# Windowed attention followed by a gated feed-forward: feed-forward in chunks of 384 tokens, q and k loaded as nine rows per partition, and jobs placed by time and dependency

## The chip, the cores and the metric

The kernel runs on one core of a Trainium2 chip. The core has five engines that run their own instruction streams in order and wait for each other through semaphores: TensorE (PE, matmuls; its weight loads are listed apart as PEld), VectorE (DVE), ScalarE (ACT), GpSimd (POOL) and SyncE (SP, which here issues DMAs). Matmuls write to PSUM[...]; ScalarE and VectorE read PSUM and write SBUF. The metric is the device time of one execution in microseconds, the median of three runs; the profile is of one more execution, and its span (282.3 us) is a little shorter than that run's device time (284.04 us).

## What is computed

Eight batches of 576 tokens with 8 heads of 64 go through attention within a window of 32 tokens to each side. The result, 512 wide, goes through a feed-forward of width 1024, whose hidden layer is gated by the sigmoid of a convolution of three taps along the tokens.

```python
# q, k, v: (8, 8, 576, 64)   w_in: (512, 1024)   conv_w: (3, 1024)   w_out: (1024, 512)
scores = q @ k.T / sqrt(64); scores[|i - j| > 32] = -1e9
x      = softmax(scores) @ v                        # heads side by side: (8, 576, 512)
h      = relu(x @ w_in)                             # (8, 576, 1024)
conv   = sum_k conv_w[k] * h[:, i + k - 1]          # zero outside the 576 tokens
out    = (h * sigmoid(conv)) @ w_out                # (8, 576, 512), float32
```

## The kernel before

Inputs arrive as fp32 and are cast to bf16 by GpSimd. Per batch, q, k and v come in five blocks of 128 tokens; a row of 64 values (256 bytes) is contiguous in both places.

```python
psum = tc.tile_pool(name="psum", bufs=4, space=PSUM)          # four slots of two banks
def load_block(dst, src, b, c, lo):
    nc.sync.dma_start(dst[s0 - lo:s1 - lo, c, :, :],
                      src[b, :, s0:s1, :].rearrange("h p d -> p h d"))
# batch 0's loads are issued first; w_in (cast while it is loaded) is asked for by GpSimd after
# the casts of q and k and the first of v; then come the loads of batch 1, w_out, batch 2 ...
def load_w_in():
    for c in range(KC): nc.gpsimd.dma_start(w_in_sb[:, c, :], moe_w_in[128*c:128*c+128, :])
```

The attention of a pair of heads g (32 pairs, four per batch) is made of jobs. TensorE transposes q and k against an identity (five matmuls each), ScalarE and VectorE copy the results out; 18 small matmuls give the scores of nine query tiles of 64; ScalarE takes the exponential, VectorE multiplies by a mask; 20 matmuls multiply by v (with a column of ones, so that the sum comes along); VectorE divides; five matmuls transpose the result.

```python
def job_tr(g, which):   # q: copy by ScalarE; k: by VectorE. 128x576 each
def job_sc(g):          # scores into two slots, exp 128x576 twice, mask 128x1152 once
def job_av(g):          # 20 matmuls into one slot, reciprocal 128x10, multiply 128x640
def job_xt(g):          # 5 transposes into one slot, copy 128x576 into xT[b][:, pr, :]
```

The feed-forward works on a whole batch, in two halves of 288 tokens in the two banks of a slot:

```python
def job_ph(b, m):       # x @ w_in, one of 8 blocks m of the hidden width
    for gg in range(2):
        for kc in range(KC):      # 4
            matmul(ps[:, gg, 0:288], w_in_sb[:, kc, m*128:(m+1)*128], xT[b][:, kc, gg*288:(gg+1)*288])
    nc.scalar.activation(hT[:, m, 1:S+1], ps, Relu, scale=0.5)
def job_pc(b, m):       # the convolution: three diagonal matrices, shifted reads of hT
    for gg in range(2):
        for kk in range(3):
            matmul(ps[:, gg, 0:288], diag_w[:, kk, m, :], hT[:, m, gg*288+kk:gg*288+kk+288])
    nc.scalar.activation(tn, ps, Tanh)                     # sigmoid by way of tanh
    nc.vector.scalar_tensor_tensor(out=gT[...], in0=tn, scalar=1.0, in1=hT[:, m, 1:S+1], add, mult)
def job_py(bp, tiles):  # gated @ w_out for one or two tiles of 128 tokens of a pair of batches
    # 8 matmuls of 512 columns per tile, one ScalarE copy, one store of up to 512 KB
```

The order in which the jobs are given out is a merge: in period `per`, the attention of batch `per`, the feed-forward of batch `per - 1` and the loads of batches `per + 1` and `per + 2` are mixed in proportion.

```python
for per in range(B + 2):
    extra = lj[1] if per == 0 else lj[per + 1][cut:] ...
    extra = extra + lj[per + 2][:cut] ...
    merge(extra, att.get(per, []), ffn.get(per, []))
```

So the feed-forward of batch 0 stands in the order beside the attention of batch 1.

Of the kernel before, what the change touches and what calls it, by code (L numbers as in the profile page):

```python
# [15 lines left out]
def kernel(  # L17
# [21 lines left out]
    TG = S // 2  # L39
    PAD = 32  # L40
    AVS = 171
# [6 lines left out]
    psum = ctx.enter_context(tc.tile_pool(name="psum", bufs=4, space=bass.MemoryType.PSUM))  # L48

    NLD = 2  # L50
    qst = pp.tile([128, NBLK, H, 64], FP32, name="qst")
    kst = pp.tile([128, NBLK, H, 64], FP32, name="kst")
    vst = pp.tile([128, NBLK, H, 64], FP32, name="vst")
    qnb_pp = [pp.tile([128, NBLK, H, 64], BF16, name=f"qnb{i}") for i in range(NLD)]
    knb_pp = [pp.tile([128, NBLK, H, 64], BF16, name=f"knb{i}") for i in range(NLD)]
# [4 lines left out]
    hT_pp = [pp.tile([128, MB, S + 2], BF16, name=f"hT{i}") for i in range(2)]  # L60
# [6 lines left out]
    mask = consts.tile([128, NT, 64], BF16, name="mask")  # L67
# [3 lines left out]
    def load_block(dst, src, b, c, lo):  # L71

        s0, s1 = max(0, lo), min(S, lo + 128)
        fixed(nc.sync.dma_start(  # L74
            dst[s0 - lo:s1 - lo, c, :, :], src[b, :, s0:s1, :].rearrange("h p d -> p h d")
        ))

# [5 lines left out]
    def load_stream(b):  # L83

        i = b % NLD
        ve, vo = ve_pp[i], vo_pp[i]

        def cast_v(c):
            cast(ve[:, c, :, 0:64], vst[:, c, :, :])
            half = cast if b > 0 else nc.scalar.copy  # L90
            if c < NBLK - 1:
                half(vo[0:64, c, :, 0:64], vst[64:128, c, :, :])
            if c > 0:
                half(vo[64:128, c - 1, :, 0:64], vst[0:64, c, :, :])

        for c in range(NBLK):
            yield (lambda c=c: load_block(qst, q, b, c, 128 * c),
                   lambda c=c: cast(qnb_pp[i][:, c, :, :], qst[:, c, :, :]))
            yield (lambda c=c: load_block(kst, k, b, c, 128 * c),
                   lambda c=c: cast(knb_pp[i][:, c, :, :], kst[:, c, :, :]))  # L100
        for c in range(NBLK):
            yield (lambda c=c: load_block(vst, v, b, c, 128 * c - PAD), lambda c=c: cast_v(c))


    for st in (qst, kst):
        nc.vector.memset(st[64:128, NBLK - 1, :, :], 0.0)
# [3 lines left out]
    for ld, _ in loads0:  # L110
        ld()
    nc.scalar.dma_start(
# [4 lines left out]
    nc.vector.memset(mask, 1.0)  # L117
    nc.gpsimd.affine_select(
        out=mask, in_=mask, compare_op=ALU.is_ge, fill=0.0, base=0,
# [3 lines left out]
        out=mask, in_=mask, compare_op=ALU.is_ge, fill=0.0, base=64,  # L123
        pattern=[[0, NT], [1, 64]], channel_multiplier=-1,
    )
    nc.vector.memset(mask[0:PAD, 0, :], 0.0)
    nc.vector.memset(mask[128 - PAD:128, NT - 1, :], 0.0)
# [5 lines left out]
    for t_ in hT_pp:  # L133
        nc.vector.memset(t_[:, :, 0], 0.0)
        nc.vector.memset(t_[:, :, S + 1], 0.0)
    for kk in range(3):
        for m in range(MB):
            nc.vector.tensor_scalar(
                out=diag_w[:, kk, m, :], in0=ident,
                scalar1=conv_w_sb[:, kk, m:m + 1], scalar2=None, op0=ALU.mult,  # L140
            )

    def load_w_in():
        for c in range(KC):
            fixed(nc.gpsimd.dma_start(w_in_sb[:, c, :], moe_w_in[128 * c:128 * c + 128, :]))

    def load_w_out():
        fixed(nc.gpsimd.dma_start(w_out_sb, moe_w_out.rearrange("(c p) f -> p c f", p=128)))


    def slot():
        return psum.tile([128, 2, 512], FP32, name="ps", tag="ps")

    def flat(ps):
        return ps.rearrange("p a x -> p (a x)")
# [4 lines left out]
    def transpose_into(ps, nat):  # L160

        pf = flat(ps)
        for c in range(NBLK):
            cols = min(128, S - 128 * c)
            nc.tensor.matmul(  # L165
                pf[:, 128 * c:128 * c + cols], nat(c), ident[:, 0:cols], start=True, stop=True
            )
        return pf[:, 0:S]

    def job_tr(g, which):  # L170
        b, pr = g // NP, g % NP
        nat = (qnb_pp if which == "q" else knb_pp)[b % NLD]
        t_ = transpose_into(
            slot(), lambda c: nat[:, c, 2 * pr:2 * pr + 2, :].rearrange("p h d -> p (h d)")
        )
        if which == "q":
            qT = apool.tile([128, S], BF16, name="qT", tag="qT")
            state["q", g] = qT
            nc.scalar.copy(out=qT, in_=t_)  # L179
        else:  # L180
            kT = kT_pp[g % NKT]
            state["k", g] = kT
            nc.vector.tensor_copy(out=kT[:, PAD:PAD + S], in_=t_)

    def job_sc(g):
        qT, kT = state.pop(("q", g)), state.pop(("k", g))
        pss = [slot(), slot()]
        for t in range(NT):
            for e in range(2):
                nc.tensor.matmul(  # L190
                    flat(pss[e])[:, 64 * t:64 * t + 64],
# [4 lines left out]
        attn = apool.tile([128, 2, S], BF16, name="attn", tag="attn")  # L196
        state["a", g] = attn
        for e in range(2):
            nc.scalar.activation(attn[:, e, :], flat(pss[e])[:, 0:S], AF.Exp, bias=0.0, scale=scale)  # L199
        nc.vector.tensor_tensor(  # L200
            out=attn, in0=attn,
            in1=mask.rearrange("p t x -> p (t x)")[:, None, :].broadcast_to([128, 2, S]),
            op=ALU.mult,
        )

    def job_av(g):
# [4 lines left out]
        pf = flat(slot())  # L211
        for c in range(NBLK):
            for e in range(2):
                for j in range(2):
                    t = min(2 * c + j, NT - 1)
                    nc.tensor.matmul(  # L216
                        pf[64 * j:64 * j + 64, AVS * c + 65 * e:AVS * c + 65 * e + 65],
                        attn[:, e, 64 * t:64 * t + 64],
# [3 lines left out]
        po = pf[:, 0:AVS * NBLK].rearrange("p (c x) -> p c x", x=AVS)[:, :, 0:130].rearrange(  # L222
            "p c (e x) -> p c e x", x=65
        )
        if pr == 0:
            xn[b] = fpool.tile([128, NBLK, H, 64], BF16, name="xn", tag="xn")
        rec = apool.tile([128, NBLK, 2], FP32, name="rec", tag="rec")
        nc.vector.reciprocal(rec, po[:, :, :, 64])
        nc.vector.tensor_tensor(  # L229
            out=xn[b][:, :, 2 * pr:2 * pr + 2, :], in0=po[:, :, :, 0:64],  # L230
            in1=rec[:, :, :, None].broadcast_to([128, NBLK, 2, 64]), op=ALU.mult,
        )

    def job_xt(g):
        b, pr = g // NP, g % NP
        t_ = transpose_into(
            slot(), lambda c: xn[b][:, c, 2 * pr:2 * pr + 2, :].rearrange("p h d -> p (h d)")
        )
        if pr == 0:
            xT[b] = fpool.tile([128, KC, S], BF16, name="xT", tag="xT")  # L240
        nc.vector.tensor_copy(out=xT[b][:, pr, :], in_=t_)  # L241
# [3 lines left out]
    def job_ph(b, m):  # L245

        hT = hT_pp[b % 2]
        ps = slot()
        for gg in range(2):
            for kc in range(KC):  # L250
                nc.tensor.matmul(  # L251
                    ps[:, gg, 0:TG],
                    w_in_sb[:, kc, m * 128:(m + 1) * 128],
# [167 lines left out]
```

The softmax here doesn't subtract the row's maximum and nothing guards it: scores larger than these inputs give would overflow.

## Time and profile before

The kernel takes 284.93 us (median; 284.92 to 285.02).

| engine | busy us | share of the span | instructions |
|---|---|---|---|
| PE | 247.8 | 88% | 2880 |
| PEld | 169.4 | 60% | 2880 |
| DVE | 164.0 | 58% | 269 |
| ACT | 159.3 | 56% | 253 |
| POOL | 130.4 | 46% | 189 |

The page of the profile cuts the span into 40 slices of 7.06 us and gives the busy share of each engine in each slice, in tenths; under these it gives the share in which the 16 DMA engines were busy and how many GB/s they moved. A TensorE that is listed as busy need not stream at its peak: matmuls overlap, and the end of each is modelled. The times from one start to the next, in a stretch without waits, tell what a matmul costs. The groups of the profile give the mean duration of an instruction of one kind; the chain of work that ended last is followed back from the last instruction, and shows what each step waited for.

### The profile page before, as it was taken

Reading aid. Unit: us, or ns where it says so; the run is one execution under the profiler, and the core shown is the slowest. Engines: PE = TensorE matmul, PEld = TensorE weight load, DVE = VectorE, ACT = ScalarE, POOL = GpSimd, SP = SyncE. Lnnn points to the kernel's source line nnn. Section 1 sums busy time; section 2 is a strip of 40 time slices with the busy share of each in tenths; the row PEclk is TensorE's granted clock in tenths of the full one; section 3 lists DMA queues with packets and bytes.
Section 4 is the critical chain, followed back from the end, with each engine's and each line's share of the span. In section 5 each row is a group of like instructions: output and inputs, shape, how many; then the busy total and the mean of one; then the engine's idle time right before and its main releaser. Section 6 shows DMA issues by size and latency. Waiting matters only on the chain.

```text
span 282.3 us, 6977 instructions
## 1 busy us (share of the span) xinstructions
PE 247.8 (88%) x2880; PEld 169.4 (60%) x2880; DVE 164.0 (58%) x269; ACT 159.3 (56%) x253; POOL 130.4 (46%) x189
## 2 busy tenths in 40 slices
PE   0356649987899999999999999999999999999994
PEld 0135526765656675767676767667567765676641
DVE  4834635686657585658665865486657735752220
ACT  1059133656556665666665766567557855575532
POOL 4583579996788358244756273736353000000000
PEclk9999999999999999999999999999999999999999
DMA  9999999999968692979858966895243010202104
GB/s 109 215 202 227 203 201 202 205 175 222 206 126 217 168 199 35 219 167 199 148 146 158 218 101 144 165 226 120 69 82 104 2 77 0 90 24 78 74 2 184
DMA packets 122175, 40.30 MB, mean 143 GB/s; under 512 B 116000, under 2 KB 117024, under 8 KB 122144
## 3 DMA queue, kind: packets, MB, share of 16 engines
q1 hardware_dynamic: 117440, 37.76, 67.1%
q0 software_dynamic: 1616, 2.10, 4.4%
q10 hardware_dynamic: 3088, 0.01, 0.7%
q8 instruction: 22, 0.36, 0.6%
q14 instruction: 9, 0.07, 0.1%
HBM read 32.52 MB, written 9.44 MB: 149 GB/s over the span
## 4 chain that ended last, share of the span: by engine, by line
PE 75%; DMA 8%; ACT 7%; SPq 4%; DVE 2%; issue 1%; POOL 1%; ACTq 0%
PE ps L251 23%; PE ps L293 22%; PE ps L269 17%; PE ps L165 6%; DMA kst<-in_k_dram 5%; ACT y_sb L300 5%; SPq L74 4%; PE ps L216 3%; PE ps L190 3%; DMA vst<-in_v_dram 2%; DMA qst<-in_q_dram 2%; ACT tn L276 1%; ACT hT_87 L257 1%; DVE gT L279 1%; ACT attn L199 1%
## 5 line engine op out<-in xcount | busy, mean ns | idle before, releaser
L251 PE MATMUL ps<-xT,w_in_sb 128*128 128x288 bf16 x512 | 75.4, 291 | 3.1 <-DVE xT L241 1.2
L293 PE MATMUL ps<-w_out_sb,gT 128*128 128x512 bf16 x288 | 65.3, 379 | 0.4 <-ACT tn L276 0.4
L251 PEld LDWEIGHTS <-w_in_sb 128*128 128x128 bf16 x512 | 47.5, 99 | 16.7 <-issue 3.6
L276 ACT ACTIVATE tn<-ps 128x576 f32<-128x576 f32 x64 | 41.8, 654 | 18.3 <-PE ps L269 17.3
L293 PEld LDWEIGHTS <-gT 128*128 128x128 bf16 x288 | 27.3, 98 | 31.0 <-DVE gT L279 0.5
L300 ACT COPY y_sb<-ps 128x1024 f32<-128x1024 f32 (+1 forms) x20 | 18.5, 927 | 46.3 <-PE ps L293 46.3
L199 ACT ACTIVATE attn<-ps 128x576 bf16<-128x576 f32 x64 | 38.4, 653 | 6.1 <-PE ps L190 6.0
L269 PEld LDWEIGHTS <-diag_w 128*128 128x128 bf16 x384 | 34.1, 97 | 9.7 <-issue 1.3
L200 DVE TENSOR_TENSOR attn<-attn,mask 128x1152 bf16<-128x1152 bf16 x32 | 25.9, 810 | 23.7 <-ACT attn L199 23.6
L279 DVE SCALAR_TENSOR_TENSOR gT<-tn,hT_88 128x576 bf16<-128x576 f32 x32 | 26.5, 831 | 19.0 <-ACT tn L276 18.8
L179 ACT CAST qT<-ps 128x576 bf16<-128x576 f32 x32 | 20.1, 637 | 22.7 <-PE ps L165 22.6
L279 DVE SCALAR_TENSOR_TENSOR gT<-tn,hT_87 128x576 bf16<-128x576 f32 x32 | 28.0, 878 | 5.3 <-ACT tn L276 5.2
L269 PE MATMUL ps<-hT_87,diag_w 128*128 128x288 bf16 x192 | 29.0, 286 | 1.2 <-ACT qT L179 0.6
L269 PE MATMUL ps<-hT_88,diag_w 128*128 128x288 bf16 x192 | 29.0, 286 | 0.0
L257 ACT ACTIVATE hT_87<-ps 128x576 bf16<-128x576 f32 x32 | 21.0, 656 | 13.0 <-PE ps L251 12.3
L257 ACT ACTIVATE hT_88<-ps 128x576 bf16<-128x576 f32 x32 | 21.0, 656 | 11.9 <-PE ps L251 11.7
L229 DVE TENSOR_TENSOR xn<-ps,rec 128x640 bf16<-128x640 f32 x32 | 26.3, 822 | 0.8
L241 DVE CAST xT<-ps 128x576 bf16<-128x576 f32 x32 | 23.7, 751 | 4.4 <-PE ps L165 4.4
L79 POOL TENSOR_SCALAR vo_83<-vst 64x512 bf16<-64x512 f32 x32 | 23.9, 748 | 2.4
L79 POOL TENSOR_SCALAR knb_79<-kst 128x512 bf16<-128x512 f32 x20 | 13.7, 684 | 22.5 <-DMA kst<-in_k_dram 17.9
L216 PEld LDWEIGHTS <-attn 128*64 128x64 bf16 x640 | 14.6, 115 | 11.8 <-issue 9.5
L79 POOL TENSOR_SCALAR ve_81<-vst 128x512 bf16<-128x512 f32 x20 | 14.0, 700 | 16.6 <-DMA vst<-in_v_dram 8.4
(64 smaller groups left out, 277.2 us busy)
## 6 DMA issues: line engine op xcount, KB each, us to landing
qst<-in_q_dram SPq DMA_DIRECT2D x32, 256.0 KB, 4.9
kst<-in_k_dram SPq DMA_DIRECT2D x32, 256.0 KB, 5.4
out_dram<-y_sb SPq DMA_DIRECT2D x16, 512.0 KB, 3.4
vst<-in_v_dram SPq DMA_DIRECT2D x24, 256.0 KB, 5.2
vst<-in_v_dram SPq DMA_DIRECT2D x16, 192.0 KB, 4.8
qst<-in_q_dram SPq DMA_DIRECT2D x8, 128.0 KB, 5.1
kst<-in_k_dram SPq DMA_DIRECT2D x8, 128.0 KB, 4.8
w_in_sb<-in_moe_w_in_dram POOLq DMA_DIRECT2D x4, 256.0 KB, 6.8
```

What stands on the lines that cost most here:

```text
L79: fixed(nc.gpsimd.tensor_scalar(out=out_, in0=in_, scalar1=1.0, scalar2=0.0, op0=ALU.mult, op1=ALU.add))
L199: nc.scalar.activation(attn[:, e, :], flat(pss[e])[:, 0:S], AF.Exp, bias=0.0, scale=scale)
L200: nc.vector.tensor_tensor(out=attn, in0=attn, in1=mask.rearrange("p t x -> p (t x)")[:, None, :].broadcast_to([128, 2, S]), op=ALU.mult,)
L229: nc.vector.tensor_tensor(out=xn[b][:, :, 2 * pr:2 * pr + 2, :], in0=po[:, :, :, 0:64], in1=rec[:, :, :, None].broadcast_to([128, NBLK, 2, ...
L241: nc.vector.tensor_copy(out=xT[b][:, pr, :], in_=t_)
L251: nc.tensor.matmul(ps[:, gg, 0:TG], w_in_sb[:, kc, m * 128:(m + 1) * 128], xT[b][:, kc, gg * TG:(gg + 1) * TG], start=(kc == 0), stop=(kc ...
L257: nc.scalar.activation(hT[:, m, 1:S + 1].rearrange("p (gg x) -> p gg x", x=TG), ps[:, :, 0:TG], AF.Relu, bias=0.0, scale=0.5,)
L269: nc.tensor.matmul(ps[:, gg, 0:TG], diag_w[:, kk, m, :], hT[:, m, gg * TG + kk:gg * TG + kk + TG], start=(kk == 0), stop=(kk == 2),)
L276: nc.scalar.activation(tn.rearrange("p (gg x) -> p gg x", x=TG), ps[:, :, 0:TG], AF.Tanh, bias=0.0, scale=1.0)
L279: nc.vector.scalar_tensor_tensor(out=gT[b // 2][:, m, b % 2, :], in0=tn, scalar=1.0, in1=hT[:, m, 1:S + 1], op0=ALU.add, op1=ALU.mult,)
L293: nc.tensor.matmul(ps[:, i, :], g_[:, m, 128 * tb:128 * tb + 128], w_out_sb[:, m, :], start=(m == 0), stop=(m == MB - 1),)
L300: nc.scalar.copy(out=y_sb[:, 0:n, :], in_=ps[:, 0:n, :])
```

## The change

- **Loads of q and k.** A partition takes nine successive tokens of a head (2,304 bytes in a row) instead of one row of 256 bytes; q goes to partitions 0 to 63 and k to 64 to 127 of one tile. One transpose then gives q and k of 128 tokens at once, and the copies out of PSUM put the tokens in order again, with a stride. v is loaded as before.
- **Weights.** w_in and w_out are loaded as fp32 by SyncE's queue, w_in right behind batch 0, w_out behind batch 1, and cast by GpSimd.
- **Feed-forward in chunks.** Two batches together are 1,152 tokens: three chunks of 384, each with one token more at an edge inside a batch for the convolution. A matmul then has 384 to 386 columns instead of 288. Chunk 1, which spans batches 0 and 1, is done in two halves.
- **PSUM.** One slot of three banks for transposes and scores (`pa`), five slots of one bank for all else (`pf`), instead of four slots of two banks. v's product takes two `pf` slots per pair of heads, and so two reciprocals and two multiplications.
- **Order.** Each job has a planned time and a list of jobs that must stand ahead of it; they are given out by time as their predecessors have been given out. The feed-forward of batch 0 is planned for 25 us. Jobs of VectorE planned before 39 us keep their place in the program's order.

The diff, cut to its core:

```diff
-    TG = S // 2
+    CH = 2 * S // 3
+    HW = CH // 2
-    psum = ctx.enter_context(tc.tile_pool(name="psum", bufs=4, space=bass.MemoryType.PSUM))
+    psum_a = ctx.enter_context(tc.tile_pool(name="psum_a", bufs=1, space=bass.MemoryType.PSUM))
+    psum_f = ctx.enter_context(tc.tile_pool(name="psum_f", bufs=5, space=bass.MemoryType.PSUM))
...
+    qkst = pp.tile([128, H, RP, 64], FP32, name="qkst")
+    def load_qk(b, pr):
+        for p0, src in ((0, q), (64, k)):
+            fixed(nc.sync.dma_start(
+                qkst[p0:p0 + 64, 2 * pr:2 * pr + 2, :, :],
+                src[b, 2 * pr:2 * pr + 2, :, :].rearrange("h (p j) d -> p h j d", j=RP),
+            ))
...
+    def load_weight(src, dst, rows, cast_):
+        ...
+                fixed(nc.sync.dma_start(st[0], src.rearrange("(c p) f -> p c f", p=128)[:, :, x:x + n]))
...
+        for js in ((range(0, 4), range(4, 8), range(8, RP)) if b < 2 else (range(RP),)):
+            ps = slot_f() if b < 2 else slot_a()
+            for j in js:
+                nc.tensor.matmul(ps[:, 128 * (j - j0):128 * (j - j0) + 128],
+                    nat[:, pr, j, :, :].rearrange("p e d -> p (e d)"), ident, start=True, stop=True)
+            rows = ps[:, 0:128 * n].rearrange("p (j y x) -> p y x j", j=n, y=2)
+            nc.scalar.copy(out=qT...[:, :, j0:j0 + n], in_=rows[:, 0])
+            vector.tensor_copy(out=kT...[:, :, j0:j0 + n], in_=rows[:, 1])
...
-        for e in range(2):
-            nc.scalar.activation(attn[:, e, :], flat(pss[e])[:, 0:S], AF.Exp, bias=0.0, scale=scale)
+        x = 2 * S - 64
+        nc.scalar.activation(attn[:, 0:x], ps[:, 0:x], AF.Exp, bias=0.0, scale=scale)
+        nc.scalar.activation(attn[:, x:], last[:, 0:64], AF.Exp, bias=0.0, scale=scale)
...
+    def job_ph(c, m, halves=(0, 1)):
+        ps = slot_f()
+        for kc in range(KC):
+            nc.tensor.matmul(ps[:, 0:n], w_in_sb[:, kc, m * 128:(m + 1) * 128], x_[:, kc, x0:x1], ...)
+    def job_pc(c, m, halves=(0, 1)):
+        ps = slot_f()
+        for kk in range(3):
+            nc.tensor.matmul(ps[:, 0:n], diag_w[:, kk, m, :], taps(kk), ...)
+    def job_py(c, i):
+        ...                                    # one tile of 128 tokens, copy 128x512, store 256 KB
...
+    P = 29.0
+    PC = 2.0 * P / 3.0
+    T0, T1 = 25.0, 47.0
+    start = {0: T0, 1: T1}
+    for c in range(2, NCH + 1):
+        start[c] = T1 + 12.0 + (c - 2) * PC
...
+        at(("tr", g), t, lambda g=g: job_tr(g), ("cast", b, g % NP), ("sc", g - 3))
+        at(("sc", g), t + x0 * d, lambda g=g: job_sc(g), ("tr", g), ("av", g - 4))
+        at(("av", g), t + x1 * d, lambda g=g: job_av(g), ("sc", g), ("av", g - 1), ...)
...
+    give_out()
```

## The prediction

> **What bounds the kernel now.** I read the 40 slices first, then the DMA part, the chain of waits, and last the stretches and groups that give the sizes.
>
> ```profile
> PE   0356649987899999999999999999999999999994
> DMA  9999999999968692979858966895243010202104
> DMA packets 122175, 40.30 MB, mean 143 GB/s; under 512 B 116000, under 2 KB 117024, under 8 KB 122144
> PE 75%; DMA 8%; ACT 7%; SPq 4%; DVE 2%; issue 1%; POOL 1%; ACTq 0%
> ```
>
> From the twelfth slice on, TensorE is busy throughout. In the eleven slices before (78 us) it is not, and there the DMA engines are full. 116,000 of the 122,175 packets are below 512 B: the 256-byte rows of q, k and v. The stretches and the chain say what that costs:
>
> ```profile
> core 0: us, PE busy (x) PEld busy (x) DVE busy (x) ACT busy (x) POOL busy (x), PEclk, DMA share, GB/s
> 20.00:30.00 10.00, 6.33 (x95) 5.03 (x93) 6.00 (x10) 7.83 (x13) 4.26 (x7) 1.00 1.21 227
> ...
> 270.00:280.00 10.00, 8.42 (x39) 3.45 (x36) 0.95 (x2) 2.91 (x4) 0.00 (x0) 1.00 0.26 103
> ```
>
> ```profile
> 22.42 9.59 DMA kst<-in_k_dram
> ...
> 46.01 1.31 PE ps L251 x5
> ...
> 113.28 1.09 PE ps L251 x8
> ...
> 172.16 1.09 PE ps L251 x8
> ```
>
> Full of 256-byte rows, the DMA gives 227 GB/s. When only 2 KB rows of the output are moved, it gives 103 at a share of 0.26, so about 390 if full. The feed-forward (L251) starts in earnest only about 46 us, after batch 1's k, though it needs batch 0 alone. The two lines at 113.28 and 172.16 are the same place two batches apart: a steady pair of batches takes 58.9 us.
>
> What TensorE must stream I take from the groups' counts and the dense runs: eight matmuls of 288 columns every 0.98 us (122.5 ns each), sixteen of 512 in 3.45 us (216 ns), a transpose of 576 columns 0.25 us, a job of scores or of the product with v about 0.37 us. Then 512 x 0.1225 = 62.7, 384 x 0.1225 = 47.0, 288 x 0.216 = 62.2, 96 transposes x 0.25 = 24.0, 64 attention jobs x 0.37 = 23.7: together **219.6 us**. The last matmul ends at about 278.5, so 59 us are lost. A steady pair of batches streams 54.9 of its 58.9 us, an efficiency of 0.93; from 84 to 250 us that is a loss of 11. The other **48 us are lost in the first 84**. That is the part worth attacking.
>
> [...] So I use 163 ns for 385 columns. [...] The new q and k transfers take 64 partitions each; nothing in this trace shows long rows into half the partitions. [...]the trace's two copies, 586 ns for 512 and 1012 for 1024, give 0.832 and a fixed 160.
>
> **The change part by part.**
>
> *TensorE's stream.* First product: 384 matmuls x 163.1 = 62.6, plus 0.1 for the halved chunk. Convolution: 288 x 162.5 = 46.8. The output product and the attention stay; q and k need 288 transposes of 128 columns instead of 320 of which some had 64, the same columns. Sum 219.6: **nothing saved**. 200 fewer matmuls give 0.5 us, and the extra edge columns take it back. So all of the gain must come from waits.
>
> *The other engines* get more instructions. ScalarE (160 + 0.832 per column): relu 47, tanh 47, exp 41, q 23, outputs 21, some xT 4: 183 instead of 159. VectorE (about 150 + 1.04 per column in rows such as 751 for 576): gates 64, multiplications of the product with v 31, reciprocals 13, mask 26, k 26, xT 23, and 17 of setup: some 200 instead of 164. In a span near 260 that is 70% and 77%: not bounds, but queues get longer. GpSimd stays near 125 (q and k 32 x 1.4, v 70, weights 10).
>
> *The start.* SyncE issues from 1.3 us. For q and k I choose 280 GB/s, between 227 and 390[...]. Batch 0: q and k 2.36 MB, 8.4 us; v 1.18 MB at about 220, 5.4; the 12 KB of conv_w in 4-byte packets about 2 (0.7% of 282 us); w_in 2.7 per half at 390. With 1.9 us to land (the 2.6 of a 256 KB store less its transfer), v is in at 17.0, and w_in at 21.7 and 24.4. The cast of a half on GpSimd (620 ns for 512 elements, so about 2.5 for 2,048) gives 24.2. Beside it: the product with v from 17.6, eight reciprocals and multiplications at 0.69, 5.5 us, and five copies of xT, about 2: 25.5. **The feed-forward starts near 25.5 instead of 43.6 us**, with 6 us streamed.
>
> *Batch 1* comes behind w_in: from 22.5, q and k take 8.4 and the last v lands near 38. But GpSimd casts v in 13 pieces of 0.7 to 0.75, 9.5 us from 34 on: the last piece is ready at 43.5. In the changed instruction order TensorE has 15.3 us of stream up to the end of batch 1's first product with v. It would get there by about 38 and waits for these casts until **44 us: 28.7 lost so far**. Behind it the order asks for batch 2 only after 7 more us of stream (about 51), when w_out and its casts are done, and for the end of batch 2's v near 67; these loads fit.
>
> *The rest.* 204.3 us remain. I choose an efficiency of 0.95: the new order puts attention jobs singly between feed-forward jobs, which should help against 0.93, while busier ScalarE and VectorE cost some of it. The last 25 us, without attention, run densely, as they do now. 44 + 179.3/0.95 + 25 = 257.7. The tail, with a smaller copy (586 instead of 1012 ns) and the store, 3.5: a span of 261. The device time is 2.6 over the span (284.9 against 282.3): 263.8; I take **262**, since the load rate is more likely too low than too high here.
>
> **The rivals.**
> 1. [...] q and k then load at about 220 GB/s, 10.8 instead of 8.4 us per batch: +2.4 at batch 0's end and as much again at batch 1's. About 267. For it: the 64-partition form. Against it: q and k of one pair are queued behind each other and may overlap.
> 2. *Evacuation becomes the bound.* Five one-bank slots at about 0.57 us of matmuls each let TensorE run some 2.9 us ahead, four two-bank slots about 4. A VectorE queue of gate, mask and copies (0.65 + 0.81 + 0.75) uses most of this. An efficiency of 0.90 instead of 0.95 costs 10 us: 272. For it: +24 and +37 us of work there, and strided reads for q and k that no row yet prices. Against it: both keep over 20% free.
> 3. *Batch 1 arrives in time.* At 390 GB/s and with casts overlapping better, the wait for v ends near 36 instead of 44: 254 to 256.
> 4. *The early start gains nothing*, because TensorE is in order and waits later for batches 2 and 3. Then steady lines would stay as they are and the time near 280. Against it: after the first 84 us the DMA share falls to 0.7 to 0.9, even with 256-byte rows.
>
> **Range and chances.** Start (25.5 ± 2.5), stall (28.7 ± 5 lost), efficiency (0.95 ± 0.03, which is ± 6 us) combine to about ± 8; the unknown price of the strided copies widens the upper side. 253 to 273. To lose the 2% it would have to be above 279: efficiency below 0.88 with nothing else won, so I give that 7%.
>
> **What would show it.** First L251-like matmul (x @ w_in) at 23 to 28 us; packets mostly 2,304 B, with v's 36,864 of 256 B left; by 44 us an idle TensorE waiting for GpSimd's v; a chunk of two-thirds of a batch every 19 to 19.5 us; VectorE near 200 busy and ScalarE near 183; PE idle naming ScalarE or VectorE as releaser if rival 2 holds; landing times of q and k of 295 KB near 3 us if full[...]. I would be wrong if the strided copies cost well over 0.8 us, or if the single `pa` slot chains transposes and scores.

## The result: 283.2 us instead of 262

The changed kernel takes 283.21 us (median of 4 runs, 282.32 to 283.58), the kernel before on the same chip 284.95: a ratio of 0.9934, interval 0.9908 to 0.996. It is 0.7% faster, and the 23 us that the prediction saw did not come. Times of the experiments below are medians, and runs more than 1.5% above the fastest of the same kernel (one of 328.57 us among them) are left out of medians and ratios. Each ratio is to the kernel before, run on the same chip beside it, so that an experiment gains over the changed kernel where its ratio lies clearly below 0.9934.

The changed kernel's 40 slices (PE, PEclk and DMA) and its packet line answer to those shown of before:

```profile
PE   0655883687999998999999999999999999999994
PEclk9999999599999999999999999999999999999999
DMA  6999999999970994469448755695610101111022
DMA packets 58160, 42.40 MB, mean 151 GB/s; under 512 B 42256, under 2 KB 44304, under 8 KB 58128
PE 66%; DVE 11%; DMA 7%; SPq 7%; POOL 4%; issue 2%; ACT 1%; POOLq 0%
```

TensorE is now 0.8 busy in slices five and six (28 to 42 us), where it was 0.4 to 0.6: the early start is there. In slice seven it drops to 0.3, and the half clock of slice eight follows. The packets are as predicted (q and k in rows of 2,304 bytes), yet the DMA engines are full to the end of slice eleven, 77 us, as they were before.

In the line of shares the chain of work that ended last shrank on TensorE from 75% to 66%, and VectorE's part grew from 2% to 11%. The chain itself, in order of time (start, duration, what), up to 55 us:

```profile
20.11 9.32 DMA wst<-in_moe_w_in_dram
29.44 10.42 DMA qkst<-in_k_dram
...
40.00 1.43 POOL qkb_79 L104
...
50.59 0.62 POOL vo_83 L104
...
51.25 0.29 PE pf L253 x3
```

L104 is the helper of GpSimd's casts, L253 the product with v, L80 the helper of VectorE. So for 31 us the chain runs through the transfers of w_in and of batch 1 and through GpSimd's casts of batch 1, and TensorE picks up again at 51.5 us, not 44.

**Where the time went.** To compare stretch by stretch I added up the prediction's price of each matmul by the time at which the trace has it start; what is missing to the clock is lost. (Where records of the output product are missing from a trace, 29 of 288 in some, I made them up in proportion.)

| stretch, us | lost before | lost after | predicted |
|---|---|---|---|
| 0 to 44 | 36.1 | 28.8 | 28.7 |
| 44 to 52 | 3.4 | 7.6 | 0.4 |
| 52 to 80 | 6.9 | 7.3 | 1.4 |
| 80 to 125 | 3.8 | 6.7 | 2.2 |
| 125 to 250 | 7.7 | 6.7 | 5.4 |
| 250 to the last matmul | 0.8 | 0.4 | 0 |

At 44 us the changed kernel is 7.3 us ahead. At 125 us it is level (50.2 and 50.4 lost). From there on it runs nearly as predicted: 118.3 us of stream in 125, an efficiency of 0.946. Of some 19 us that were lost and not predicted, 7.2 lie between 44 and 52 us and 10.4 between 52 and 125 us. The steps before 44 us failed too, but their errors cancel in this sum (see below).

### The profile page after: what moved, and what is told of

It reads as the page before. It is cut to its first block, busy times and chain, and to the rows that moved or that the text cites. A ratio compares the mean times of both kernels' runs of the same rounds, so it can differ in the third digit from the quotient of the medians.

```text
span 280.6 us, 6798 instructions
## 1 busy us (share of the span) xinstructions
PE 246.3 (88%) x2680; PEld 148.1 (53%) x2680; DVE 184.5 (66%) x400; ACT 171.4 (61%) x363; POOL 115.4 (41%) x140
## 4 chain that ended last, share of the span: by engine, by line
PE 66%; DVE 11%; DMA 7%; SPq 7%; POOL 4%; issue 2%; ACT 1%; POOLq 0%
PE pf L361 22%; PE pf L305 19%; PE pf L343 14%; DMA qkst<-in_k_dram 4%; PE pa L207 4%; PE pf L253 3%; DMA wst<-in_moe_w_in_dram 3%; SPq L91 3%; DVE gT L80 3%; PE pa L228 3%; POOL vo_83 L104 2%; DVE attn L80 2%; DVE xn L80 2%; SPq L98 2%; PE pf L275 2%
## 5 line engine op out<-in xcount | busy, mean ns | idle before, releaser
L305 PE MATMUL pf<-xT,w_in_sb 128*128 128x385 bf16 (+2 forms) x416 | 81.9, 322 | 3.0 <-DVE xT L80 2.4
L361 PE MATMUL pf<-w_out_sb,gT 128*128 128x512 bf16 x288 | 68.1, 380 | 0.3
L347 ACT ACTIVATE tn<-pf 128x384 f32<-128x384 f32 (+1 forms) x104 | 49.6, 477 | 15.7 <-PE pf L343 14.7
L80 DVE TENSOR_TENSOR attn<-attn,mask 128x1152 bf16<-128x1152 bf16 x32 | 28.6, 893 | 23.9 <-ACT attn L238 23.1
L361 PEld LDWEIGHTS <-gT 128*128 128x128 bf16 x288 | 27.3, 98 | 28.7 <-DVE gT L80 0.2
L237 ACT ACTIVATE attn<-pa 128x1088 bf16<-128x1088 f32 x32 | 34.6, 1081 | 2.7 <-PE pf L228 2.0
L80 DVE SCALAR_TENSOR_TENSOR gT<-tn,hT_88 128x384 bf16<-128x384 f32 (+1 forms) x40 | 25.9, 654 | 11.2 <-ACT tn L347 11.0
L104 POOL TENSOR_SCALAR qkb_78<-qkst 128x1152 bf16<-128x1152 f32 x16 | 19.5, 1217 | 29.0 <-DMA qkst<-in_k_dram 18.1
L80 DVE TENSOR_TENSOR xn<-pf,rec 128x320 bf16<-128x320 f32 x64 | 30.1, 488 | 1.0
L104 POOL TENSOR_SCALAR qkb_79<-qkst 128x1152 bf16<-128x1152 f32 x16 | 19.5, 1219 | 26.7 <-DMA qkst<-in_k_dram 26.0
L253 PEld LDWEIGHTS <-attn 128*64 128x64 bf16 x640 | 16.1, 117 | 22.8 <-issue 17.5
L80 DVE SCALAR_TENSOR_TENSOR gT<-tn,hT_89 128x384 bf16<-128x384 f32 x32 | 20.0, 629 | 12.3 <-ACT tn L347 12.0
L80 DVE CAST xT<-pf 128x512 bf16<-128x512 f32 (+1 forms) x34 | 21.0, 636 | 6.8 <-PE pf L275 6.7
L80 DVE SCALAR_TENSOR_TENSOR gT<-tn,hT_87 128x384 bf16<-128x384 f32 x32 | 20.1, 630 | 6.0 <-ACT tn L347 6.0
L104 POOL TENSOR_SCALAR vo_83<-vst 64x512 bf16<-64x512 f32 x32 | 22.9, 716 | 2.4
L343 PE MATMUL pf<-hT_88,diag_w 128*128 128x384 bf16 (+1 forms) x120 | 22.6, 295 | 0.0
L343 PE MATMUL pf<-hT_87,diag_w 128*128 128x384 bf16 x96 | 21.4, 333 | 0.7 <-DVE xn L80 0.7
L343 PE MATMUL pf<-hT_89,diag_w 128*128 128x384 bf16 x96 | 20.9, 326 | 0.0
```

The costliest lines, as they stand in the source:

```text
L80: ins = getattr(nc.vector, name)(*args, **kwargs)
L104: fixed(nc.gpsimd.tensor_scalar(out=out_, in0=in_, scalar1=1.0, scalar2=0.0, op0=ALU.mult, op1=ALU.add))
L237: nc.scalar.activation(attn[:, 0:x], ps[:, 0:x], AF.Exp, bias=0.0, scale=scale)
L253: nc.tensor.matmul(pss[e][64 * j:64 * j + 64, 65 * c:65 * c + 65], attn[:, col(e, t):col(e, t) + 64], (ve if t % 2 == 0 else vo)[:, t // 2 ...
L305: nc.tensor.matmul(ps[:, 0:n], w_in_sb[:, kc, m * 128:(m + 1) * 128], x_[:, kc, x0:x1], start=(kc == 0), stop=(kc == KC - 1),)
L343: nc.tensor.matmul(ps[:, 0:n], diag_w[:, kk, m, :], taps(kk), start=(kk == 0), stop=(kk == 2))
```

## Experiments

### The arrival of batch 1: casts on another engine, k on another queue

My first theory (A): GpSimd's casts of batch 1's v hold TensorE at 45.6 to 51.5 us. The rival (B): VectorE, 9.7 of 10 us busy from 60 to 70 us, holds it. A third, that q and k in long rows into 64 partitions come at no more than about 220 GB/s, is the prediction's own first rival.

```diff
-(cast if b > 0 else vector.tensor_copy)(vo[0:64, c, :, 0:64], vst[64:128, c, :, :])
+(vector.tensor_copy if b == 0 else nc.scalar.copy if b == 1 else cast)(vo[0:64, c, ...
```

> Edit: the eight half-casts of batch 1's v (64x512 each) go from GpSimd to ScalarE; nothing is left out. Theory A (the wait for batch 1's v casts on GpSimd, 45.6 to 51.5 us in the changed kernel, is what ate the lead that TensorE has at 44 us): GpSimd is done with batch 1's v at about 45 to 46 instead of 51.2 us, the wait shrinks to 1 us or less, TensorE keeps its full clock, and 5 to 8 us of 283.2 stay: 275 to 278. Theory B (VectorE bounds the stretch from 52 to 110 us): TensorE goes on earlier, but VectorE sets the pace, and by 110 us nothing is left: above 281.

Measured: 282.05 us, ratio 0.9892 (0.9848 to 0.9937), not to be told from the changed kernel. TensorE's waits from 44 to 53 us in the changed kernel, and from 44 to 54 in this run (waiting engine, its line, what it waited for: us, times, longest):

```profile
PE pf L253 <- POOL vo_83 L104: 6.3, 4, 1.9
```

```profile
PE pf L253 <- ACT vo L118: 4.9, 4, 1.8
```

The wait changed its engine and stayed. In this run v landed between 41.2 and 46.1 us, yet ScalarE's eight copies ran from 45.1 to 51.6 us: in its order they stood behind an exponential and a tanh of other jobs, with more of these between them. The first and the last of them:

```profile
45.14 1.14 ACT L116 CAST vo<-vst 64x512 bf16<-64x512 f32 x2
...
50.49 1.14 ACT L118 CAST vo<-vst 64x512 bf16<-64x512 f32 x2
```

The edit made the copies no earlier, so it does not test theory A.

```diff
-fixed(nc.sync.dma_start(qkst[p0:p0 + 64, ...
+fixed((nc.scalar if p0 and b < 2 else nc.sync).dma_start(qkst[p0:p0 + 64, ...
```

> Edit: the k loads of batches 0 and 1 are issued on ScalarE's DMA queue, so that q (partitions 0 to 63) and k (64 to 127) can be moved at the same time. [...]the four pairs of batch 0 are cast at about 9 to 10 us instead of 14.0, the first matmul of x @ w_in comes at 27 to 28.5 instead of 31.3, GpSimd finishes batch 1's v at 44 to 47 instead of 51.2; with theory A 275 to 279. If the engines' rate for 2,304-byte rows is the limit, the fourth cast stays at 14 us and the time at 283.

Measured: 278.15 us from three runs, ratio 0.9758 (0.9692 to 0.9825): the clearest gain of any single edit. With conv_w in rows besides, below, it is not seen again.

```diff
-vector.tensor_scalar(out=diag_w[:, kk, m, :], in0=ident, scalar1=conv_w_sb[...], ...)
+nc.scalar.activation(diag_w[:, kk, m, :], ident, AF.Copy, bias=0.0, scale=conv_w_sb[...])
-    at(("diag", m), T0 + 1.6 * m - 1.0, ...
+    at(("diag", m), T0 - 4.5 + 0.1 * m, ...
```

> Edit: the 24 diagonal matrices of the convolution (8 us of VectorE between 31 and 56 us) are made by ScalarE, idle from 20.5 to 29.8 us. Theory B (VectorE bounds the ramp): 5 to 8 us of VectorE's queue vanish and the time falls to 277 to 280. Theory A: the wait for v stays until 51.5, only the 2.7 us of matrices behind it go: 281 to 282.5.

> Edit: the first and the third together (batch 1's half-casts of v and the diagonal matrices on ScalarE). If A and B both hold, the gains add: 271 to 276. If what is won in the ramp is lost again behind it (loads of batches 2 and 3, or VectorE's queue up to 110 us), no better than the better of the two alone, and TensorE's stream at 110 us stands where it stood.

Measured: 281.62 (ratio 0.9885, 0.9827 to 0.9942), and both edits together 281.94 (0.9903, 0.987 to 0.9936). Taking 8.0 us of diagonal matrices off VectorE leaves the stop at 46 to 52 us as it was. So B alone does not make this stop. In the run with both edits ScalarE's copies of v again ended late, at 51.2 us, so the sum of A and B is not tested either.

### Is it the supply? conv_w, and a batch that need not come

The trace has a hole in the supply. Stretches of the changed kernel (us, then busy time and count of each engine, granted clock, DMA share, GB/s):

```profile
6.00:10.00 4.00, 1.14 (x9) 0.88 (x9) 1.20 (x3) 1.18 (x3) 2.30 (x2) 1.00 1.03 235
18.00:20.00 2.00, 1.58 (x23) 1.09 (x24) 1.40 (x3) 1.43 (x4) 0.82 (x2) 1.00 1.33 21
22.00:26.00 4.00, 2.25 (x54) 1.87 (x54) 3.22 (x11) 0.00 (x0) 1.34 (x1) 1.00 1.05 403
```

Long rows of q and k into 64 partitions come at 235 GB/s, hardly faster than the 227 of 256-byte rows before. 2 KB rows of w_in into 128 partitions come at 403. Between them the 3,072 four-byte packets of conv_w keep the engines full (a share of 1.33) while they move 21 GB/s. Theory S: the first 80 us are bound by this supply.

The next four runs take the supply apart. The first leaves out the 13 loads of batch 1 (its casts read what batch 0 left, so its output is not the reference's). The second (the second diff) loads conv_w as 24 rows and turns them with one matmul. The third joins this with k on ScalarE's queue. The fourth adds matmuls that nobody reads:

```diff
-at(("load", b, i), x, ld if b else lambda: None, ...
+at(("load", b, i), x, ld if b > 1 else lambda: None, ...
```

```diff
-nc.sync.dma_start(conv_w_sb, bass.AP(..., [[1, 128], [d_ff, 3], [128, MB]]))   # after v
+nc.scalar.dma_start(cw_nat, moe_conv_w.rearrange("k (m p) -> (k m) p", p=128))  # first
+nc.scalar.copy(out=cw_b, in_=cw_nat)
+nc.tensor.matmul(cw_ps[:, 0:24], cw_b, ident[0:24, 0:24], start=True, stop=True)
+nc.scalar.copy(out=conv_w_sb..., in_=cw_ps[:, 0:24])
```

```diff
 # job_av(g)
+if g == 8:
+    dps = slot_f()
+    for _ in range(24):
+        nc.tensor.matmul(dps, w_in_sb[:, 0, 0:128], w_in_sb[:, 1, 0:512], start=True, stop=True)
 pss = [slot_f(), slot_f()]
```

> The eight q and k loads and five v loads of batch 1 are left out (3.5 MB); the casts of batch 1 read what batch 0 left in the staging tiles, so batch 1's output is not the reference's. Everything else stands. Theory S (the first 80 us are bound by how fast batches arrive): batch 1's casts can start when w_in is cast, near 30 us, so v of batch 1 is ready at about 43 us instead of 51.2, the wait at 45.6 to 51.5 and the half clock after it go; lost time at 52 us falls from 36.4 to 30 or less, and the time to 270 to 275. Theory V (VectorE, 9.7 of 10 us busy from 60 to 70, bounds the stretch behind the wait whatever arrives): the wait goes but comes back as waits for VectorE before 80 us; lost time at 80 us stays within 2 us of 43.7 and the time above 279.

> conv_w is fetched first, on ScalarE's queue, as 24 rows of 512 bytes, turned by one matmul into its 128 x 24 form; the 3,072 packets of 4 bytes between v and w_in are gone. Theory S: w_in's casts start 2 to 3 us earlier (24.7 becomes about 22), the feed-forward starts at 28.5 to 29.5 instead of 31.3, batch 1's v is ready 2 us earlier than 51.2, and the time falls by 2 to 3 us to about 280 to 281. Rival: the hole only delays what is waited for anyhow by GpSimd; the time stays at 283.

> Both: k of batches 0 and 1 on ScalarE's queue beside q on SyncE's, and conv_w as in the run before it. Theory S: the gains add, 278.8 less 2 to 3 us, so about 276; q/k casts of batch 0 follow each other faster than one in 2.6 us, the feed-forward starts at about 27 us, batch 1's v is ready by about 45 us. Theory V: no more than the better of the two alone, 278 to 279.

> 24 matmuls of 512 columns whose result nobody reads (5.2 us at full clock) stand ahead of batch 1's first product with v, inside the wait at 45.6 to 51.5 us. If the half clock from 49.6 to 56.4 us, seen after that wait, costs what it seems to (some 3 us of stream at half speed), the time falls by 1.5 to 3 us to 280 to 281.5 and the granted clock stays 1.0 in 50 to 56. If VectorE holds TensorE there anyhow, the clock stays full and the time at 283.

Measured: 281.83 us without batch 1's loads (0.991, 0.9877 to 0.9943), 281.47 with conv_w in rows (0.9868, 0.9825 to 0.9911), 281.84 with k's queue besides (0.9895, 0.9843 to 0.9948). Theory S in its plain form falls: a batch that need not be waited for is worth 1.4 us by median, which is not clear of noise. This run also tests theory A: batch 1's v was cast by 44.4 us, so the wait for it is not the whole cause. The run shows why. VectorE in it, from 44 us on, then GpSimd, then TensorE (start, duration, engine, line, operation, in brackets the wait before it):

```profile
45.29 1.98 DVE L80 TENSOR_TENSOR attn<-attn,mask 128x1152 bf16<-128x1152 bf16 x1 [0.38 <-ACT attn L238]
47.20 4.12 DVE L80 TENSOR_SCALAR diag_w<-ident,conv_w_sb 128x128 bf16<-128x128 bf16 x3
```

```profile
44.49 4.54 POOL L104 TENSOR_SCALAR w_out_sb<-wst 128x2048 bf16<-128x2048 f32 x2
49.00 4.89 POOL L104 TENSOR_SCALAR qkb<-qkst 128x1152 bf16<-128x1152 f32 x4
```

```profile
52.46 1.14 PE L343 MATMUL pf<-hT,diag_w 128*128 128x384 bf16 x3 [5.84 <-DVE xn L80]
```

v is there, and TensorE stops from 46.6 to 52.5 us all the same (xn, which it waits for, stands behind these in VectorE's queue). GpSimd, no longer waiting for v, went on to the long casts of w_out and of batch 2. During these three diagonal matrices took VectorE 4.12 us and a mask 1.98. In the run with early diagonals below, those beside which GpSimd was idle took 0.24 each; a mask without a cast beside it takes 0.76. So when the first cause of the stop at 46 us is taken away, **a second one of the same length takes its place**. (In the changed kernel itself w_out is cast from 51.3 to 55.0 us, behind the stop; the edit moved these casts forward.)

In the kernel with k's queue and conv_w in rows, TensorE was granted 0.69 of its clock from 30 to 60 us in the profiled run; why, I can't say. The run that was to keep the clock missed its place: the unread matmuls stood ahead of batch 2's first product with v (pair 8), not batch 1's (pair 4). It took 285.04 us (1.0014, 0.9995 to 1.0034): 5.2 us of added matmuls cost 1.8, so TensorE was idle for some 3 us there.

### Both at once, the clock, and GpSimd kept quiet

With conv_w here by about 3 us, the diagonals can be built while VectorE has nothing else. The first run does that on top of conv_w in rows, the second leaves out batch 1's loads besides, the third has k's queue instead, and the fourth is the changed kernel with the unread matmuls at `g == 4`:

```diff
-    at(("diag", m), T0 + 1.6 * m - 1.0, ...
+    at(("diag", m), 3.0 + 1.0 * m, ...
```

> conv_w as 24 rows, fetched first, and the 24 diagonal matrices built by VectorE at 3 to 16 us, where it was idle, instead of 24 to 40 us. Theory D (two bounds lie on top of each other from 30 to 70 us, the arrival of batch 1 and VectorE's queue, and lifting one only uncovers the other): batch 1's v still comes at 49 to 51 us, so little is won over the run with conv_w in rows alone: 279 to 281.5. Theory V (VectorE alone): 274 to 277. Theory S (arrival alone): 281 to 282.

> The same, and the loads of batch 1 left out as before (its casts read batch 0's staging; its output is not the reference's). Theory D: now both bounds are lifted together; the sum is far more than the parts (1.4 us for the loads alone, 1.7 us for conv_w alone): 268 to 275, and lost time at 80 us falls from 43.7 to 36 or less. If neither bounds it (TensorE's order, the clock, or GpSimd's casts do), the time stays above 278.

> The early diagonals with k of batches 0 and 1 on ScalarE's queue: both bounds eased by something that the whole computation allows. Theory D: below both parts, 275 to 278.5. If the clock takes it back (in the run with k's queue and conv_w in rows the granted clock was 0.58 to 0.76 in 30 to 60 us), 280 or more with a clock below 0.9 there.

> In the run called keep_clock the 24 unread matmuls stood ahead of batch 2's first product with v, not batch 1's as meant. Here they stand ahead of batch 1's (5.2 us at full clock, inside the wait at 45.6 to 51.5 us). Clock theory: the half clock at 49.6 to 56.4 goes, 280 to 282. If VectorE paces TensorE there, the clock stays full and the time 283 to 284.

Measured: early diagonals 280.08 us (0.9834, 0.9786 to 0.9882), clearly below the changed kernel; with k's queue 279.8 (0.9821, 0.9759 to 0.9884), no clear step beyond. With the loads of batch 1 left out besides, the four times spread from 276.1 to 283.3 us; this run decides nothing.

The clock alone gains nothing. Stretches of the changed kernel, then of the run with unread matmuls ahead of batch 1's v (clock is the third figure from the end):

```profile
44.00:52.00 8.00, 1.37 (x19) 0.91 (x19) 2.27 (x7) 1.07 (x3) 7.23 (x11) 0.77 1.07 333
52.00:60.00 8.00, 6.72 (x75) 3.97 (x76) 7.89 (x19) 4.81 (x13) 6.10 (x5) 0.80 1.09 228
60.00:70.00 10.00, 8.27 (x140) 6.88 (x140) 9.68 (x23) 6.92 (x21) 8.20 (x12) 1.00 1.11 215
```

```profile
44.00:52.00 8.00, 7.51 (x57) 3.74 (x56) 3.31 (x8) 2.71 (x7) 7.30 (x10) 1.00 1.07 318
52.00:60.00 8.00, 5.74 (x75) 3.42 (x76) 7.90 (x17) 5.01 (x13) 6.43 (x5) 1.00 1.08 228
60.00:70.00 10.00, 7.59 (x134) 6.33 (x134) 9.37 (x23) 6.32 (x19) 7.27 (x11) 1.00 1.09 209
```

The clock stays at 1.00, and the time at 283.11 us (0.9951, 0.9929 to 0.9973). TensorE has done 20.1 us of useful stream at 60 us with them and 20.2 without, and VectorE is busy for 7.9 of 8 us from 52 to 60 in both: behind the wait VectorE sets the pace, and a faster TensorE only waits for it. The opposite relief looks just as worthless: in the run with the diagonals on ScalarE, VectorE was busy for 7.1 of these 8 us, but TensorE was busy from 52 to 56 us at a clock of 0.50 and again had 20.2 us at 60:

```profile
52.00:56.00 4.00, 3.97 (x30) 1.78 (x30) 3.78 (x10) 0.98 (x2) 4.00 (x3) 0.50 1.05 240
```

Early diagonals took both away (the clock was 1.00 throughout the profiled run): TensorE had 22.8 us at 60, 2.6 more. What the clock is worth once VectorE is out of the way, no run shows apart.

So the next question was VectorE itself, and whether GpSimd makes it slow (theory G). I sorted VectorE's instructions in the changed kernel by whether a GpSimd cast covered them (over 60% of their time) or not (under 10%):

| instruction | its inputs | alone | with GpSimd |
|---|---|---|---|
| mask (576 x 2) | two in SBUF | 0.76 (15) | 1.08, up to 1.67 (12) |
| gate (384) | two in SBUF | 0.55 (55) | 0.80, up to 1.42 (21) |
| diagonal matrix (128) | one in SBUF, one scalar per partition | 0.25 (12) | 0.64, up to 1.47 (9) |
| division of the product with v | one in PSUM | 0.49 (34) | 0.49 (26) |
| xT, k from PSUM | one in PSUM | 0.69, 0.75 | 0.69, 0.75 |

So VectorE's instructions whose inputs all lie in SBUF are stretched under a GpSimd cast: the mask from 0.76 to 1.08 us, the gate from 0.55 to 0.80, the diagonal matrix, with one such input and a scalar, from 0.25 to 0.64. Those with an input in PSUM are not: 0.49, 0.69 and 0.75 us with and without a cast. What makes the difference, no run shows. In the kernel before, where GpSimd's casts of q and k were 512 elements and not 1,152, the 32 masks averaged 810 ns; they now average 893. But the stretched instructions do not lie in the ramp alone. Of 18 gates of 384 columns that took over 0.6 us, five come before 110 us and 13 after, up to 207 us, where the kernel runs at 0.946. So a stretched instruction need not cost time, and the table alone does not prove theory G.

The first of these four adds to early diagonals and missing loads that GpSimd's casts of batch 1 are left out (batch 1 reads batch 0's q, k and v). The second moves the shifted copy of v by transfers:

```diff
-(cast if b > 0 else vector.tensor_copy)(vo[0:64, c, :, 0:64], vst[64:128, c, :, :])      # 8 per batch
+nc.gpsimd.dma_start(vo[0:64, :, :, :], ve[64:128, 0:NBLK - 1, :, :])                     # 2 per batch
+nc.gpsimd.dma_start(vo[64:128, :, :, :], ve[0:64, 1:NBLK, :, :])
```

The third cuts GpSimd's long casts, and the fourth joins the shift with early diagonals, conv_w in rows and k's queue:

```diff
-cast(qkb_pp[i][:, pr, :, :, :].rearrange("p j e d -> p e j d"), qkst[:, 2 * pr:2 * pr + 2, :, :])
+[cast(qkb_pp[i][:, pr, :, e, :], qkst[:, 2 * pr + e, :, :]) for e in range(2)]
-cast_(dst[:, :, x:x + n], st[0])
+[cast_(dst[:, r:r + rows // 4, x:x + n], st[0][:, r:r + rows // 4, :]) for r in range(0, rows, rows // 4)]
```

> As the run with early diagonals and no loads of batch 1, and GpSimd's casts of batch 1 are left out too: batch 1 reads batch 0's q, k and v (its output is not the reference's). Theory G (VectorE is slowed by GpSimd's casts): from 30 to 45 us VectorE's gates take 0.55 to 0.6 and its masks 0.76 us, the stretches that lost 1.5 to 3.4 us there go, and the time falls from 281.7 to 268 to 275. Rival O (TensorE's own order, with later batches arriving at the same pace, gives every early gain back): 278 or more.

> The changed kernel with one edit: the shifted copy of v is no longer cast a second time (38.7 us of GpSimd, 3.9 of VectorE) but moved by two transfers of 64 x 4,160 bytes per batch from the first copy, on GpSimd's own queue. The whole computation stands. Theory G: GpSimd's busy time falls from 115 to below 85, VectorE's total from 184.5 to 172 or less as its gates and masks are less disturbed, batch 1's v is complete near 48.5 instead of 51.2: 276 to 279. Rival O: 281 to 283.5.

> The changed kernel with GpSimd's casts of q and k cut in two (1,152 to 576 elements) and those of the weights in four (2,048 to 512); nothing else. Theory G, in the form that VectorE waits for whole GpSimd instructions: masks that took up to 1.67 us take at most 1.4, VectorE's total falls by 3 to 6 us, and the time by 1 to 3 us to 280 to 282. If the overlap alone counts and not the length: VectorE's total within 2 us of 184.5 and the time 283 to 284.

> All that the whole computation allows together: k of batches 0 and 1 on ScalarE's queue, conv_w in rows, early diagonals, v shifted by transfers. Theory G: the first feed-forward product at 27 to 29 us, batch 1's v by 45, VectorE 165 to 172 busy: 268 to 275. Rival O: 277 to 280, no better than the early diagonals with k's queue alone (279.8).

Measured: with GpSimd quiet 276.07 us (0.9667, 0.9608 to 0.9727), 1 us above theory G's range and below rival O's. Against early diagonals alone (280.08) that is 4.0 us for everything that batch 1's loads and casts cost. It takes two things away at once, so it does not prove how much of this is VectorE's stretched instructions. Even so its gates before 110 us were still stretched, by the casts of batch 2 and 3. And it started its feed-forward late, at 35.3 us. TensorE's largest wait from 20 to 50 us in it:

```profile
PE pf L258 <- DVE vo L80: 5.8, 4, 2.0
```

vo is the shifted copy of batch 0's v, made by VectorE (L258 is the product with v here). Five of these copies took 5.41 us beside GpSimd's casts of w_in, and 2.13 in the changed kernel, where the first cast of w_in began only after them. No run moved these copies.

The shift by transfers is slower, 288.81 us (1.0116, 1.0048 to 1.0185), though GpSimd's busy time fell to 84.6 as expected, and VectorE's to 174.9. TensorE's waits from 20 to 62 us:

```profile
PE pf L253 <- DMA vo<-ve: 17.2, 2, 11.4
```

The transfers of v stand in line with everything else in DMA engines that are full up to some 80 us: one wait of 11.4 and one of 5.8 us. From 125 to 260 us, where they land in time, this kernel loses 7.4 us and the changed one 6.8: relief of VectorE and GpSimd is worth nothing there. Joined with the other edits it gives a ratio of 0.9898 (0.9799 to 0.9996), spoiled by the same wait: rival O's side, but for a reason of its own.

Short casts: 281.84 us (0.9873, 0.9817 to 0.9929), where the changed kernel's interval overlaps. Masks covered by a cast fell from 1.08 to 0.86 us, up to 1.28; VectorE's total stayed (184.7), GpSimd's rose to 125.9. Here the length of one GpSimd instruction mattered to the instruction that met it, not to the sum.

### VectorE's load from 60 to 125 us, and the best version

```diff
-(vector.tensor_copy if b > 1 or c % 2 else nc.scalar.copy)(out=xT...
+(vector.tensor_copy if b > 3 or b == 0 and c % 2 else nc.scalar.copy)(out=xT...
```

> The run with early diagonals (280.1), and besides it twelve copies of xT of batches 1 to 3 on ScalarE instead of VectorE (12 x 0.69 = 8.3 us off VectorE between about 50 and 100 us, 7.0 onto ScalarE, which is 60 to 75% busy there). Theory V2 (VectorE's own load paces 60 to 125 us): the loss from 60 to 125 us falls from 9.9 to 7 or less, the time to 276 to 278. If TensorE's own order or the arrival of batches 2 and 3 paces it: 279.5 to 281.

> The same with k of batches 0 and 1 on ScalarE's queue and GpSimd's casts cut short; the whole computation is done. If the easings add: 274 to 277. If each only uncovers the next limit: 278 to 281, within 1 us of the better of its parts (278.8 with k's queue alone).

Measured: 279.78 us (0.984, 0.9804 to 0.9876) with xT of batches 1 to 3 on ScalarE, against 280.08 without. VectorE's busy time from 60 to 125 us fell from 50.2 to 42.8, and the loss in that stretch stayed (9.9 and 9.8 us). Theory V2 falls: the sum of VectorE's work alone does not pace that stretch. (ScalarE took the work over and rose from 43.4 to 48.0 us there.)

All easings together (early diagonals, conv_w in rows, k's queue, short casts, xT on ScalarE) take **276.99 us (0.9729, 0.968 to 0.9777)**, 2.7% below the kernel before and, by the two ratios, 2.1% below the changed one, with the whole computation. It is not shown to beat k's queue alone (278.15): their intervals overlap. The rate of the first transfers of q and k tells what the second queue does; early diagonals with all on SyncE's queue, then with k on ScalarE's:

```profile
6.00:10.00 4.00, 1.39 (x12) 1.13 (x13) 3.03 (x11) 1.19 (x3) 2.37 (x2) 1.00 1.04 231
```

```profile
6.00:10.00 4.00, 1.14 (x9) 0.88 (x9) 3.75 (x13) 1.35 (x4) 1.78 (x2) 1.00 1.05 288
```

By the first two slices of the two pages, each of about 7 us, the second queue brings nothing in the first (168 GB/s with one queue, 165 with two), and the kernels move 220 and 263 in the second.

## Why the prediction was wrong, step by step

**Right.** TensorE's stream of 219.6 us is unchanged. The steady efficiency of 0.95 was measured as 0.946 from 125 us on; rival 2, evacuation at 0.90, did not come there. Busy times were predicted at 183, 200 and 125 for ScalarE, VectorE and GpSimd and measured at 171.4, 184.5 and 115.4: high, but in proportion. VectorE's strided copies of k cost 0.75 us, inside the 0.8 that I had named as the limit. Two prices of single instructions held as well: the 163 ns for a matmul of 385 columns, an estimate that lies on the line through the measured 122.5 for 288 and 216 for 512, was 164 (median from one start to the next, 194 pairs of the changed kernel's trace), and VectorE's 150 + 1.04 per column, 682 and 416 ns for 512 and 256, was 685 and 412 in the copies of xT.

**Right by luck.** The loss up to 44 us (28.7) was measured as 28.8. I had let TensorE start at 25.5, run out of work by 38 and wait for v until 44. It started at 31.3, and its waits for v (6.3 us in all, up to 51.5) began just at 44.0. A late start took the place of an early wait, and the sums are equal. A small error in the other direction: I put the device time 2.6 us above the span, from two different executions; of one and the same it is 1.7 (284.04 and 282.3 before, 282.32 and 280.6 after).

**The rate of q and k, chosen as 280 GB/s, failed.** It was 235, and the last of batch 0's k landed at 13.9 us instead of 11.6; rival 1, with about 220, had the rate. The 280 was an estimate of mine between the measured 227 and 390, which I had preferred to rival 1 because q and k of a pair might overlap; nothing in the trace before showed that. With both on one queue the rate from 6 to 10 us was 235 (231 with early diagonals), with k on a second queue 288.

**The start at 25.5 failed: it was 31.3, and the step is VectorE's chain.** Batch 0's v landed at 19.7 us (17.0 predicted). I had let the product with v begin at 17.6 and had not priced that VectorE first makes the shifted copies of batch 0's v; the last of these ended at 23.7. VectorE in the changed kernel:

```profile
21.58 2.13 DVE L80 CAST vo_82<-vst 64x512 bf16<-64x512 f32 x5
24.28 0.20 DVE L80 RECIPROCAL rec<-pf 128x5 f32<-128x5 f32 x1 [0.58 <-PE pf L253]
...
29.88 1.29 DVE L80 CAST xT<-pf 128x512 bf16<-128x512 f32 x2 [0.49 <-PE pf L275]
```

From 24.3 us on the chain ran as priced: reciprocals and multiplications to 29.4, xT to 31.2. The landing of w_in failed as well (24.6 and 29.4 instead of 21.7 and 24.4), but it did not set the start: its first half, enough for the first four blocks, was cast by 26.6, and no wait of TensorE up to there names it. Moving conv_w forward let w_in be cast earlier, onto the copies of v, and the start moved to 33.4 us in the run with early diagonals.

**Batch 1's v at 43.5 failed by 7.7 us.** It was ready at 51.2 (0.4 us predicted as lost from 44 to 52, 7.6 measured). The supply was late, not the casts: the second half of w_in landed 5.0 us late, q and k behind it took 10.5 us instead of 8.4, and the last v landed at 45.6 instead of 38. GpSimd was done 5.6 us after that, as predicted (5.5). And behind this wait stood a second limit that the prediction did not have, VectorE under GpSimd's casts; it moved forward where the wait was taken away.

**The efficiency of 0.95 from 44 us on was given to a stretch that does not have it.** From 52 to 125 us 3.6 us of loss were predicted and 14.0 measured, the largest failed term. I took the steady figure for a stretch in which the plan puts the eight attention pairs of batches 2 and 3 into some 45 us behind the rest of batch 1's, GpSimd casts w_out and two batches, and VectorE's instructions with two SBUF inputs may be stretched under these casts. That these make the loss is argued, not shown: no run changed the plan there. The kernel before loses 10.7 there with its own order, and I could have read that: I had counted it among the 48 us of the first 84 without asking which of them an earlier start removes.

**Rival 4 described the outcome**, with 280 us, but not its cause. It had TensorE wait later for batches 2 and 3. The runs show one limit behind another instead, up to 60 us: batch 1's v, then VectorE under GpSimd's casts, which move into the same microseconds when v comes early, and most single reliefs gained no more than 2 us by median.

**What stays open.** With batch 1 neither loaded nor cast, and with early diagonals, 276.1 us are left, 14 more than predicted. By the count of the table above, 3.6 of these were lost up to 44 us, in the late start behind VectorE's copies of v; 2.3 from 44 to 52; 5.9 from 52 to 125; and some 2 behind that. In the changed kernel, from 80 to 125 us, the waits that the trace names for TensorE add to 2.1 of the 6.7 us lost. The rest lies in gaps inside stretches counted as busy. It is not VectorE's sum of work alone (the run with xT on ScalarE), not the clock alone (the run with unread matmuls), not the arrival of batch 1 alone. How much of it is VectorE's stretched instructions, how much the planned order, and how much the price of changing between attention and feed-forward jobs, no run here tells apart.

## What to carry to other kernels

Starting a stage earlier is worth what the stages behind it don't take back: before counting the gain, ask of every later stretch what bounds it, and take the loss of the kernel before in that same stretch rather than its steady efficiency. A second limit that moves into the place of the first makes each single relief look worthless; take both away before judging either. And where GpSimd casts, price VectorE's instructions with two SBUF inputs, and its copies and scalings within SBUF, by their disturbed time, not by the fastest one in the trace: here a mask took 1.08 us under a cast and 0.76 without, a gate 0.80 and 0.55, a diagonal matrix 0.64 and 0.25, and five copies of v 5.41 and 2.13.

## What the hardware showed that I had not expected

- VectorE under GpSimd's casts: three 128 x 128 scalings, 0.24 us each where GpSimd was idle, took 4.12 us under casts of 1.2 to 2.3 us; instructions that read PSUM took 0.49, 0.69 and 0.75 us with a cast and without, the same to 0.01 us.
- Two queues into the two halves of the partitions brought more than one: 231 GB/s with q and k on one queue, 288 on two, from 6 to 10 us, 25% in that stretch; over the first two slices of the pages, about 14 us, it was 194 and 214, 10%.
- 3,072 packets of four bytes (12 KB) kept the 16 DMA engines full from 18 to 20 us (a share of 1.33), in which they moved 21 GB/s in all.
- A granted clock of 0.77 to 0.80 around a wait of 6 us cost nothing here (283.1 us with it kept at 1.00, 283.2 without), where VectorE set the pace behind the wait.
